# Order of four w3 transfers and of one V transfer in a one-core decode kernel

## The chip, the cores and the metric

The kernel runs on one core of a Trainium2 chip. A core has a matrix engine (PE, with its weight loads shown as PEld), a vector engine (DVE), an activation engine (ACT), GpSimd (POOL) and a sync engine (SP), and 16 DMA engines that bring data from HBM into its on-chip memory of 128 partitions. DMAs are issued by instructions on SP, ACT or POOL. The metric is the time of one execution on the device in microseconds, lower is better. The time before is 530.65 us, the median of three runs (530.46 to 531.92).

## What is computed

One decode step of a transformer block for four sequences, with attention and a gated feed-forward part in parallel on the same normalised input, both added to x:

```python
x = A_x                                   # 4 x 1 x 640, bf16
xn = _layernorm(x)
# attention: 32 heads of 192, the last W = 2048 of 8192 cached positions
q = x @ wq                                # 640 x 6144
scores = einsum("bhqd,bhkd->bhqk", q, k) * 192 ** -0.5
o = einsum("bhqk,bhkd->bhqd", softmax(scores), v)
attn = o.reshape(B, Sq, 6144) @ wo        # 6144 x 640
# feed-forward
h = silu(xn @ w1) * (xn @ w3)             # w1, w3: 640 x 1536
ffn = h @ w2                              # 1536 x 640
return x + attn + ffn
```

There is little arithmetic for each byte: the windows of K and V are 3 MiB per head each, 64 such tiles, and each byte is used once.

## The kernel before

**Tiles.** For one head, K and V of the window are tiles of 128 partitions (32 position groups by 4 sequences) of 64 positions by 192 numbers, 24,576 bytes in a partition. `load_k` and `load_v` bring one tile each by a DMA issued on SP; `load_v` can cut it into parts along the positions. There are two K buffers and three V buffers, so K of head h waits until the four multiplies on K of head h-2 are done, and V of head h until the matmuls of `pv` for head h-3 are done.

**Work on a head.** It is cut into four units, 128 in all (NU). For each unit DVE multiplies a quarter of K with the broadcast query (`mult`, line 246), PE adds up over slices of the head dimension with an identity matrix (`adder`, line 257), DVE reduces to scores (`reduce_quarter`, line 265). Four units on, a short chain gives the maximum, the exponentials and the masked weights z (lines 269 to 301); `pv` (line 309) is 32 matmuls of z with V, and `ge_sum`, `ge_turn` and `ge_proj` (lines 334 to 348 and 233) sum, divide, turn and project with wo, a group of four heads at a time.

**Order.** The order of instructions on each engine is written by hand: `add(slot, phase, function, ...)` puts work into a slot, and the loop at the end emits the slots in order, within a slot by phase. Issues of DMAs have phase 0. SP executes its issues in that order, and an issue that waits for its buffer holds those behind it. K of head h is issued in slot 4(h-1), V of head h in slot 4h+2, up to head 28. The last ones are different. K31 is in slot 120 (NU-8), V29 in slot 121 (NU-7), and slot 122 (NU-6) has V30, V31 in two parts, the first part of w2, the last two parts of wo and two small parts of w2. So SP's order at the end is K29, V28, K30, K31, V29, V30, V31a, V31b, w2, wo, wo, w2, w2.

**w3.** w1 comes early on SP. w3 comes through GpSimd's queue in slot 24, into the buffer of w1, as four DMAs (`ffn_load_split`, lines 362 to 370). A reset of the queue's cursor goes first. The 640 rows of w3 are spread unevenly over the partitions: partitions 0 to 63 hold four rows each, partitions 64 to 127 hold six. `SPLIT` (line 184) has the two kinds in the order four, six; each DMA fills 32 partitions, and the source is viewed as 8 by 4 partitions. So the four DMAs are: four rows to partitions 0 to 31 (384 KB), six rows to 64 to 95 (576 KB), four rows to 32 to 63, six rows to 96 to 127. The matmuls that read w3 (line 377) are in slot 31. The first part of w2 uses the same buffer after it.

## Time and profile before

| what | value |
|---|---|
| median of three runs | 530.65 us |
| the profiled execution, whole | 530.28 us |
| its span, first to last instruction | 528.5 us |
| bytes moved by DMA, mean rate | 223.31 MB, 423 GB/s |
| busy share of the span | PE 68%, DVE 66%, PEld 27%, ACT 8%, POOL 1% |
| chain that ended last | DMA 65%, DVE 22%, PE 11%, ACT 1% |
| median time from issue to landing | K 18.8 us, V 26.3 us |

The profile is of one execution. Its lists say, for every instruction, when it started, how long it took, and what ended the idle time before it. The chain of waits goes back from the last instruction, at each step to what released it. Views by windows give, for a stretch of the span, each engine's busy time, the granted PE clock, the busy share of the 16 DMA engines (a packet counts where it starts, so a short window can show over 1) and GB/s. DMA queues have numbers: q1 is SP's, q0 is GpSimd's, q10 is ACT's, q8 and q14 carry instructions. The trace also has a record of each DMA packet (start, duration, bytes, queue), which does not name the DMA engine.

### The profile page before, as it was taken

The numbers are of one execution on the slowest core, as the hardware profiler recorded it, in microseconds if no ns is written. First come the engines' busy times: TensorE is split into PE (matmuls) and PEld (weight loads), VectorE is DVE, ScalarE is ACT, GpSimd is POOL, SyncE is SP. The second block draws the span as 40 slices with busy tenths as digits, with TensorE's granted clock in tenths as the row PEclk, the third lists the DMA queues.
The fourth block names the chain that finished last, engine by engine and source line by source line (L and its number), as shares of the span: only waits on it lengthen the run. The fifth ranks groups of instructions, "written<-read, shape, count | busy, mean of one in ns | idle before, by whom it ended". The sixth has DMA issues, their size and how long they took to land.

```text
span 528.5 us, 5466 instructions
## 1 busy us (share of the span) xinstructions
PE 358.2 (68%) x2316; PEld 142.8 (27%) x2317; DVE 346.8 (66%) x445; ACT 44.3 (8%) x142; POOL 3.4 (1%) x12
## 2 busy tenths in 40 slices
PE   2766638686756766667738768576686867685774
PEld 1322213232222322222213323232232322232232
DVE  4179545787577767686646877477657876776940
ACT  2121000000000000000000000000000000000010
POOL 0001000000000000000000000000000000000000
PEclk9989787889878999798897988799878898889999
DMA  8999999999999999999999999999999999999995
GB/s 358 435 427 440 417 432 443 424 438 427 432 433 430 433 428 433 429 433 431 432 435 430 430 430 432 432 435 432 433 423 439 427 435 427 435 429 400 422 406 214
DMA packets 11888, 223.31 MB, mean 423 GB/s; under 512 B 1484, under 2 KB 1624, under 8 KB 2776
## 3 DMA queue, kind: packets, MB, share of 16 engines
q1 hardware_dynamic: 11528, 221.00, 97.7%
q0 software_dynamic: 320, 1.97, 0.9%
q8 instruction: 18, 0.29, 0.2%
q14 instruction: 6, 0.05, 0.0%
q10 hardware_dynamic: 16, 0.01, 0.0%
HBM read 222.96 MB, written 0.01 MB: 422 GB/s over the span
## 4 chain that ended last, share of the span: by engine, by line
DMA 65%; DVE 22%; PE 11%; ACT 1%; issue 1%; SPq 0%
DMA kt<-in_A_k_cache_dram 55%; DVE pr L246 15%; DMA w<-in_B_w_dram 6%; PE ps L257 6%; DMA wt<-in_A_wq_dram 4%; DVE sc L265 3%; PE po L334 2%; PE qps L212 1%; DVE z L301 1%; ACT ex L293 1%; DVE oT L342 1%; PE mt L287 0%; DVE og L339 0%; DVE qbc L218 0%; PE mt L274 0%
## 5 line engine op out<-in xcount | busy, mean ns | idle before, releaser
L257 PE MATMUL ps<-pr,idb 128*128 128x512 bf16 x768 | 215.5, 423 | 148.3 <-DVE pr L246 148.2
L246 DVE TENSOR_TENSOR pr<-kt,qbc 128x3072 bf16<-128x3072 bf16 x128 | 223.4, 1746 | 109.0 <-DMA kt<-in_A_k_cache_dram 109.0
L257 PEld LDWEIGHTS <-idb 128*128 128x128 bf16 x768 | 75.6, 103 | 256.1 <-issue 200.1
L265 DVE TENSOR_REDUCE sc<-ps 128x16 f32<-128x512 f32 x128 | 87.1, 681 | 2.4 <-PE ps L257 2.4
L309 PE MATMUL o_ps<-vt,z 128*8 128x384 bf16 x1024 | 56.2, 351 | 0.6 <-DMA vt<-in_A_v_cache_dram 0.6
L334 PE MATMUL po<-o_sb,sel_w 128*32 128x192 f32 x128 | 49.2, 518 | 1.1 <-ACT o_sb L316 1.1
L309 PEld LDWEIGHTS <-z 128*8 128x8 bf16 x1024 | 25.2, 90 | 30.1 <-issue 19.5
L316 ACT COPY o_sb<-o_ps 128x384 f32<-128x384 f32 x32 | 15.3, 478 | 189.0 <-PE o_ps L309 189.0
L301 DVE TENSOR_TENSOR z<-ex,mask_b 128x256 bf16<-128x256 bf16 x32 | 13.5, 422 | 23.9 <-ACT ex L293 23.9
L290 ACT COPY negm<-mt 128x1 f32<-128x1 f32 x32 | 5.1, 159 | 244.5 <-PE mt L287 244.5
L334 PEld LDWEIGHTS po<-o_sb,sel_w 128*32 128x32 f32 x128 | 13.8, 130 | 28.7 <-issue 26.9
L212 PE MATMUL qps<-wt,xnT 128*128 128x512 bf16 x59 | 16.1, 429 | 3.4 <-DMA wt<-in_A_wq_dram 3.3
L218 DVE CAST qbc<-qps 128x512 bf16<-128x512 f32 x6 | 3.8, 684 | 16.3 <-PE qps L212 16.3
L279 DVE TENSOR_REDUCE gmax<-mt 1x4 f32<-1x128 f32 x32 | 8.8, 275 | 6.9 <-PE mt L274 6.9
L287 PEld LDWEIGHTS mt<-ones_ff,gneg 1*128 1x128 f32 x64 | 9.4, 182 | 13.8 <-issue 10.4
L287 PE MATMUL mt<-ones_ff,gneg 1*128 1x1 f32 x64 | 12.1, 256 | 0.0
L274 PE MATMUL mt<-idf,lmax 128*1 128x128 f32 x32 | 11.2, 351 | 1.1 <-DVE lmax L269 1.1
L293 ACT ACTIVATE ex<-sc,negm 128x64 bf16<-128x64 f32 x32 | 11.1, 348 | 1.0
L233 PE MATMUL acc<-wo_t,oT 128*4 128x320 bf16 x96 | 9.2, 298 | 2.3 <-DMA wo_t<-in_A_wo_dram 2.3
L212 PEld LDWEIGHTS <-xnT 128*128 128x128 bf16 x60 | 6.4, 107 | 12.7 <-issue 7.6
L321 PEld LDWEIGHTS po<-rsum,tot_w 128*32 128x32 f32 x64 | 4.5, 108 | 13.3 <-issue 12.7
L269 DVE TENSOR_REDUCE lmax<-sc 128x1 f32<-128x64 f32 x32 | 7.0, 220 | 1.1
(63 smaller groups left out, 67.6 us busy)
## 6 DMA issues: line engine op xcount, KB each, us to landing
kt<-in_A_k_cache_dram SPq DMA_DIRECT2D x32, 3072.0 KB, 18.8
vt<-in_A_v_cache_dram SPq DMA_DIRECT2D x31, 3072.0 KB, 26.3
wo_t<-in_A_wo_dram SPq DMA_DIRECT2D x8, 960.0 KB, 20.8
wt<-in_A_wq_dram SPq DMA_DIRECT2D x2, 3072.0 KB
vt<-in_A_v_cache_dram SPq DMA_DIRECT2D x2, 1536.0 KB, 31.8
w<-in_B_w_dram SPq DMA_DIRECT2D x1, 1920.0 KB, 37.0
wt<-in_A_wq_dram SPq DMA_DIRECT2D x1, 1536.0 KB, 19.9
w<-in_B_w_dram SPq DMA_DIRECT2D x1, 1280.0 KB, 34.4
```

Of the source, the lines that this page charges most:

```text
L212: nc.tensor.matmul(qp[:], lhsT=xnT[:, kc].rearrange("p a b -> p (a b)"), rhs=wq_rows[kc][:, (c0 + i) * QC:(c0 + i + 1) * QC], start=(kc == ...
L233: nc.tensor.matmul(acc[i * CT:i * CT + B, :], lhsT=lhsT, rhs=rhs[:, i * N0:(i + 1) * N0], start=first, stop=last)
L246: nc.vector.tensor_tensor(out=pr[:], in0=kts[h][:, g * JQ:(g + 1) * JQ, :], in1=qbc[:, h * Dh:(h + 1) * Dh].unsqueeze(1).to_broadcast([P, ...
L257: nc.tensor.matmul(ps[:], lhsT=idb[:], rhs=pr[:, :, kk * DD:(kk + 1) * DD], start=(kk == 0), stop=(kk == NK - 1))
L265: nc.vector.tensor_reduce(out=scs[h][:, g * JQ:(g + 1) * JQ], in_=pss.pop(u)[:], axis=AX.X, op=ALU.add)
L274: nc.tensor.transpose(out=mt[0:1, 0:P], in_=chs[h][0][:], identity=idf[:])
L287: nc.tensor.matmul(mt[:, P:P + 1], lhsT=gneg[:].rearrange("o p b -> o (p b)"), rhs=ones_ff[0:1, 0:1], start=True, stop=True)
L293: nc.scalar.activation(out=ex[:], in_=scs.pop(h)[:], func=ACTF.Exp, bias=negm[:, 0:1], scale=SCALE, accum_out=rsum[:])
L301: nc.vector.tensor_tensor(out=z[:], in0=ex[:].unsqueeze(2).to_broadcast([P, NJ, B]), in1=mask_b[:].unsqueeze(1).to_broadcast([P, NJ, B]), ...
L309: nc.tensor.matmul(o_ps[c * CT:c * CT + 2 * B, :], lhsT=z[:, 2 * jj:2 * jj + 2, :], rhs=vt[:, 2 * jj:2 * jj + 2, :], start=(jj < 4), stop= ...
L316: nc.scalar.copy(out=o_sb[:], in_=o_ps[:])
L334: nc.tensor.matmul(po[sl, 0:Dh], lhsT=sel_w[:, par].rearrange("p a b -> p (a b)"), rhs=o_sb[:, par * Dh:(par + 1) * Dh].rearrange("p (r i) ...
```

## The change

Two things are reordered; no instruction computes anything else.

- `ffn_load_split` goes through `SPLIT` in reverse order, so that the first and third of GpSimd's four DMAs are the six-row parts (partitions 64 to 95 and 96 to 127) and the second and fourth are the four-row parts.
- `load_v` takes a range of positions. V29 is loaded in two halves: the first in slot 118 (4 x 29 + 2), ahead of K31 in slot 120, the second in slot 121, where the whole of V29 was. V30 and V31 keep their places and their parts. SP's order at the end becomes K29, V28, K30, V29a, K31, V29b, V30, V31a, V31b, w2, wo, wo, w2, w2.

```diff
-    def load_v(h, parts=1):
-        vt = vpool.tile([P, NJ, Dh], BF16, tag="vt")
+    def load_v(h, j0=0, j1=NJ):
+        if j0 == 0:
+            vts[h] = vpool.tile([P, NJ, Dh], BF16, tag="vt", name="vt")
         src = v_win[:, h].rearrange("b (p j) d -> p b j d", p=PB)
-        n = NJ // parts
-        for j in range(0, NJ, n):
-            nc.sync.dma_start(out=vt[:, j:j + n, :].rearrange("q j d -> q (j d)"),
-                              in_=src[:, :, j:j + n, :].rearrange("p b j d -> p b (j d)"))
-        vts[h] = vt
+        nc.sync.dma_start(out=vts[h][:, j0:j1, :].rearrange("q j d -> q (j d)"),
+                          in_=src[:, :, j0:j1, :].rearrange("p b j d -> p b (j d)"))
...
         for g in range(HP // CT):
-            for p0, d0, kn in SPLIT:
+            for p0, d0, kn in SPLIT[::-1]:
...
-        if h < H - 2:
-            add(u0 + 2 if h < H - 3 else NU - 7, 0, load_v, h)
+        if h < H - 3:
+            add(u0 + 2, 0, load_v, h)
+        elif h == H - 3:
+            add(u0 + 2, 0, load_v, h, 0, NJ // 2)
+            add(NU - 7, 0, load_v, h, NJ // 2, NJ)
...
-    for h in range(H - 2, H):
-        add(NU - 6, 0, load_v, h, 1 + (h == H - 1))
+    add(NU - 6, 0, load_v, H - 2)
+    add(NU - 6, 0, load_v, H - 1, 0, NJ // 2)
+    add(NU - 6, 0, load_v, H - 1, NJ // 2, NJ)
```

## The prediction

> **What bounds the kernel now.** I read the page first: the DMA slices are full from end to end, and DVE at 66% and PE at 68% are far from it.

> ```profile
> DMA  8999999999999999999999999999999999999995
> ...
> q1 hardware_dynamic: 11528, 221.00, 97.7%
> q0 software_dynamic: 320, 1.97, 0.9%
> q8 instruction: 18, 0.29, 0.2%
> ```

> The reader sees the bound in the first line, and in the others who shares the 16 DMA engines: the SP queue (q1) with nearly all bytes, the four w3 transfers of GpSimd (q0), and 18 fetches of instructions (q8). Next the chain of waits (start, us, what):

> ```profile
> 480.16 11.83 DMA kt<-in_A_k_cache_dram
> 492.01 32.52 DMA w<-in_B_w_dram
> 524.58 0.73 PE acc L233 x8
> ```

> The last three steps are the landing of K31, the landing of the last part of w2 at 524.58, and PE work of 0.7 us. So the end follows the last DMA. How evenly that last DMA ends is in the windows view of half microseconds (the last two columns are the busy share of the DMA engines and GB/s):

> ```profile
> 520.50:521.00 0.50, 0.00 (x0) 0.00 (x0) 0.00 (x0) 0.00 (x0) 0.00 (x0) 1.00 0.96 389
> 521.00:521.50 0.50, 0.33 (x6) 0.24 (x7) 0.00 (x0) 0.00 (x0) 0.00 (x0) 1.00 0.72 284
> 521.50:522.00 0.50, 0.50 (x10) 0.29 (x7) 0.00 (x0) 0.00 (x0) 0.00 (x0) 1.00 0.45 184
> ...
> 522.50:523.00 0.50, 0.00 (x0) 0.00 (x0) 0.00 (x0) 0.00 (x0) 0.00 (x0) 1.00 0.37 146
> ...
> 523.50:524.00 0.50, 0.50 (x10) 0.31 (x11) 0.00 (x0) 0.00 (x0) 0.00 (x0) 1.00 0.12 49
> ...
> ```

> Up to 521 us nearly all engines work, at 521.75 seven of 16 (0.45), at 522.75 six, in the last microsecond two (0.12). Two engines set the end, over 3 us behind the first. The question is what made them late.

> **A ledger of the 16 engines.** The trace keeps each DMA packet's start, duration, bytes and queue, not its engine. The engines can be strung together all the same: a 24,576-byte packet takes 912 ns, the next on its engine starts 3 to 4 ns before its end, and every engine must meet its share (8 of 128 rows, then a 4-byte packet) of each SP transfer in the order of issue. That gives 16 unbroken chains; chains may be confused where two run in step, so halves are safer than single engines. They show:
> - Each w3 transfer lies on eight engines only: the four-row parts (12,288-byte packets, 460 ns, four per engine and transfer) on one half, the six-row parts (18,432 bytes, 686 ns) on the other. Two transfers of four packets at 0.226 us more make that half 8 x 0.226 = 1.81 us late. I call the halves light and heavy.
> - A 16,384-byte fetch holds its engine 0.95 us and lengthens its neighbour from 0.91 to 1.39, 1.42 us in all (at 299.9 us, for one). The 18 fetches go round eight engines, six heavy and two light. An 8,192-byte fetch (q14) costs 0.83.
> - Except at one place the chains show no gap above 0.15 us between 20 us and the end, so lateness stays. When K30's share lands, measured from the engine furthest ahead (478.98 us in the span), the light half is late by 0, 0.12, 0.13, 0.53, 0.86, 2.29, 2.93 and 2.98 us, the heavy one by 2.15, 2.84, 4.89, 4.95, 5.04, 5.05, 5.07 and 5.35. Two heavy engines get one more fetch after that, at 496.8 and 516.6 us.
> - The one place is where K31 waits for its buffer: the light engines have run dry.

> ```profile
> 479.00:481.00 2.00, 1.01 (x7) 0.59 (x7) 1.73 (x2) 0.00 (x0) 0.00 (x0) 1.00 0.69 295
> 481.00:483.00 2.00, 2.00 (x35) 0.81 (x34) 0.00 (x0) 0.00 (x0) 0.00 (x0) 1.00 0.88 319
> ...
> ```

> From K30's landing to the end of w2 an engine that never idles takes 39.03 us (the heavy engine with 5.35: 484.33 to 523.36). The model's last engine is then 478.98 + 5.07 + 39.03 + 1.42 = 524.50; the trace has 524.59. The ledger closes within 0.1 us.

> **The change, part by part.**
> *w3's order.* The same four transfers and bytes. If the halves follow the position in the sequence, the light half now carries 1.81 us more and the heavy one 1.81 less. Lateness at K30: 1.81, 1.93, 1.94, 2.34, 2.67, 4.10, 4.74 and 4.79 on the first half, and 0.34, 1.03, 3.08, 3.14, 3.23, 3.24, 3.26 and 3.54 on the second. With a last fetch of 1.42 on those of 3.24 and 3.26 the second half ends at 4.68, so 4.79 on the first is last. Its end is 478.98 + 4.79 + 39.03 = 522.80, against 524.50 by the same sum: 1.70 us earlier. w3 itself landed by 72 us and is read at 145.8 us, so its own landing has 73 us of cover.

> [...]

> [...]

> *Half of V29 ahead of K31.* V29's buffer is free when pv of head 26 is done, at 471.2 us (the PE matmuls of 468.94), after K30's issue at 466.69 and before the light engines run dry at 479. So V29a issues with no wait of its own that delays K31, whose release is the multiply ending at 480.1. V29a costs each engine 8 x 0.457 = 3.66 us, which fills the gap (dry from 479.3, K31's first packets at 481.6). This ends the idling of engines that are not last, so it is worth 0 at the end; the 16 half packets for eight whole ones and one more 4-byte packet cost 16 x 0.4565 - 8 x 0.9083 = 0.04 us. From both sides: the two rows above lose 2 x 0.31 + 2 x 0.12 = 0.86 us of all engines' time, the most that filling them could bring if the last engine were among the idle ones (none of the late ones has a gap there); and the 12,288-byte packets of V31a ran 0.66 us slow as a group while those of V31b did not, so at worst two halves cost 1.3. I take 0.05, nearest to V31b's row and the w3 rows.

> *What K31 delays.* K31's bytes now queue behind V29a. The last engine's K31 lands at 478.98 + 4.79 + 3.66 + 7.27 = 494.7; a multiply starts 0.42 us after its landing (484.33 to 484.75), so 495.1.

> ```profile
> 484.75 1.76 DVE L246 TENSOR_TENSOR pr<-kt,qbc 128x3072 bf16<-128x3072 bf16 x1 [4.01 <-DMA kt<-in_A_k_cache_dram]
> ...
> 493.86 1.75 DVE L246 TENSOR_TENSOR pr<-kt,qbc 128x3072 bf16<-128x3072 bf16 x1
> ...
> 496.13 1.75 DVE L246 TENSOR_TENSOR pr<-kt,qbc 128x3072 bf16<-128x3072 bf16 x1
> ```

> K31's first multiply is at 496.13. K30 lands 0.56 earlier (5.35 becomes 4.79), which moves it to 495.6, so K31 is 0.4 us early: no new wait. V29 whole lands at 478.98 + 4.79 + 14.6 = 498.4, before its matmuls at 504.5. The w2 issues that wait for earlier landings (at 492.0 and 500.4 before) move by under 3 us, ahead of packets due at 519.

> *The sum.* Span 528.5 - 1.70 + 0.05 = 526.8 us; the 3.9 us from last landing to end stay. The profiled execution took 530.28, so 528.6; the median of the runs, 530.65, is 0.37 above that: 528.9 us, 0.32% less.

> **The rivals.**
> (1) *The halves follow the partitions.* For it: partitions 0 to 63 got the four-row parts and 64 to 127 the six-row parts, so today's packets can't tell the two readings apart. Against it: line 364 resets a cursor ahead of the four transfers, which would be idle if nothing moved on with each. Time: 530.65 + 0.05 = 530.7.
> (2) *The fetches go round from another place.* 18 fetches on eight engines leave two with a third one. If one falls on a fetching engine of the first half, that ends at 4.79 + 1.42 = 6.21, i.e. 524.2 against 524.5: 530.65 - 0.3 = 530.4. For it: one of the three runs shown, 531.92, is 1.3 above the others, about one fetch. Against: the other three executions lie within 0.4 us.
> (3) *The slower one: the fetching engines are really in the light half.* My chains name no engine; if the fetches and the six-row parts are on opposite halves today, the swap puts them together and the last engine gains the whole 1.81: 530.65 + 1.81 = 532.5. It decides as soon as the engine that lands last belongs to today's light half. For it: only the stringing of chains tells. Against: fetches on the light half last 881 to 886 ns and the others 921 to 967, two kinds that fit the halves exactly, and a tail of seven engines over 1 us long is what a heavy half with fetches would leave.

> **How the numbers follow.** Forecast 0.68, (1) 0.11, (2) 0.09, (3) 0.12. The forecast's own range is 528.0 to 529.6 (half a microsecond for the runs' scatter, 0.66 once for slow half packets). A measurement can tell 0.3%, 1.6 us: below 529.06 is faster. The forecast lies 0.15 us under that bound; a fast fetch order or less scatter brings more, so I give it 0.53 faster and 0.15 same. With (1) and (2) same is 0.35, slower is (3), 0.12. The range reaches from 528.0 to 530.9 over (1) and (2) and leaves out (3).

> **What would show it.** Right: the w3 packets of 18,432 bytes come first on q0; no share under 0.9 between 479 and 483 us; the last landing near 522.9 with more than two engines busy in its last microsecond; the multiply of 496.13 not waiting for K31. Wrong: a tail as long as before with the last landing at 524.6 (1 or 2) or 526 (3), or DVE idle for K31 by more than 0.5 us.

## The result, and the profile after

The kernel after takes 539.94 us (median of 6 runs, 537.14 to 540.19); the kernel before, run beside it, 530.35. The ratio is 1.0166, 95% interval 1.0143 to 1.019: 8.8 us slower, where 1.7 us faster was forecast. The profiled execution took 540.19 us, its span 538.4.

The page of after shows where. The slices are 13.46 us each:

```profile
DMA  8999999999999999999999999999999999999994
GB/s 356 433 436 407 285 268 419 436 434 436 422 438 428 433 430 432 434 427 428 431 432 433 435 435 427 435 436 422 434 429 433 434 433 428 433 436 431 428 421 183
...
q0 software_dynamic: 320, 1.97, 1.4%
```

The engines are as busy as before, from end to end. But in slices 4 to 6 (40 to 81 us) they move 407, 285 and 268 GB/s, where every later slice but the last is at 419 or more. Measured against 430, (23 + 145 + 162) x 13.46 / 430 = 10.3 us are lost there, which covers the whole loss. GpSimd's queue moved the same 320 packets and 1.97 MB, but they held 1.4% of the engines' time instead of 0.9%. The windows view of that stretch (the last two columns are the share and GB/s), first before, then after:

```profile
50.00:60.00 10.00, 3.47 (x42) 1.60 (x42) 5.15 (x6) 0.48 (x1) 0.00 (x0) 0.88 1.00 430
60.00:70.00 10.00, 8.11 (x30) 3.04 (x29) 8.17 (x11) 0.60 (x3) 0.00 (x0) 0.78 1.01 432
70.00:80.00 10.00, 3.86 (x41) 1.54 (x39) 3.36 (x4) 0.48 (x1) 0.00 (x0) 0.73 1.00 425
```

```profile
40.00:50.00 10.00, 7.20 (x49) 3.14 (x47) 9.50 (x11) 1.75 (x3) 2.27 (x4) 1.00 1.01 433
50.00:60.00 10.00, 5.72 (x46) 2.09 (x44) 3.29 (x4) 1.10 (x4) 0.00 (x0) 0.83 1.01 293
60.00:70.00 10.00, 5.08 (x13) 1.58 (x13) 6.32 (x8) 0.00 (x0) 0.00 (x0) 0.51 1.01 304
70.00:80.00 10.00, 6.12 (x53) 2.74 (x52) 3.98 (x5) 1.08 (x4) 0.00 (x0) 0.97 1.05 270
80.00:90.00 10.00, 1.60 (x4) 0.54 (x4) 3.38 (x4) 0.00 (x0) 0.00 (x0) 0.54 0.98 409
```

A share of 1.0 at two thirds of the rate (1.01 at 293 GB/s, where it was 1.00 at 430) goes with packets that last longer. In the packet records the w3 packets start between 51.0 and 80.6 us (before: 50.6 and 70.7). The 18,432-byte packets took 686 to 1,298 ns, median 1,136, where before all took 686; the 12,288-byte packets 576 to 872, median 778, where before they took 460 to 464. The 24,576-byte packets of K and V beside them are as bad, with a median of 1,442 ns instead of 912. So it isn't w3 alone that is slow: nine of ten packets that run with it are.

DVE is where the delay is felt. Its waits for K in the timeline (in brackets the idle time and what ended it) are 9.15 and 10.96 us there, where the same two were 4.85 and 6.64. The multiply is line 246 of the kernel before and line 244 of the kernel after; before comes first:

```profile
57.88 1.76 DVE L246 TENSOR_TENSOR pr<-kt,qbc 128x3072 bf16<-128x3072 bf16 x1 [4.85 <-DMA kt<-in_A_k_cache_dram]
...
76.61 1.76 DVE L246 TENSOR_TENSOR pr<-kt,qbc 128x3072 bf16<-128x3072 bf16 x1 [6.64 <-DMA kt<-in_A_k_cache_dram]
```

```profile
63.11 1.76 DVE L244 TENSOR_TENSOR pr<-kt,qbc 128x3072 bf16<-128x3072 bf16 x1 [9.15 <-DMA kt<-in_A_k_cache_dram]
...
86.58 1.76 DVE L244 TENSOR_TENSOR pr<-kt,qbc 128x3072 bf16<-128x3072 bf16 x1 [10.96 <-DMA kt<-in_A_k_cache_dram]
```

From there on the delay is carried. By the chains of packets, the first part of wo has landed on its last engine at 78.4 us before and 88.4 after; K30 at 484.3 and 494.3. The end of the chain of waits:

```profile
476.12 22.12 DMA vt<-in_A_v_cache_dram
498.26 34.12 DMA wo_t<-in_A_wo_dram
532.42 2.85 PE acc L231 x20
535.30 0.48 DVE res L475
```

The last packet of w2 ends at 533.54 (524.59 before), 8.95 later, so the last stretch gave back 1.0 us of the ten. PE then took the microsecond away again: twenty matmuls in 2.85 us, because the granted clock was 0.50 there against 1.00 before.

The stretch around K31, where the second edit works, went as forecast:

```profile
479.00:481.00 2.00, 0.00 (x0) 0.00 (x0) 0.90 (x1) 0.00 (x0) 0.00 (x0) 1.00 1.01 426
481.00:483.00 2.00, 1.09 (x6) 0.49 (x6) 1.97 (x4) 0.00 (x0) 0.00 (x0) 1.00 1.00 430
```

The same work comes ten microseconds later in this kernel, but its 488 to 496 us are full too, with shares of 0.93 to 1.05: nothing idles ahead of K31.

### The profile page after: what moved, and what is told of

Read it like the earlier page. It is cut to its first block, busy times and chain, and to the rows that moved or that the text cites. A ratio compares the mean times of both kernels' runs of the same rounds, so it can differ in the third digit from the quotient of the medians.

```text
span 538.4 us, 5467 instructions
## 1 busy us (share of the span) xinstructions
PE 360.2 (67%) x2316; PEld 143.7 (27%) x2317; DVE 346.6 (64%) x445; ACT 44.4 (8%) x142; POOL 3.4 (1%) x12
## 3 DMA queue, kind: packets, MB, share of 16 engines
q1 hardware_dynamic: 11672, 221.00, 97.1%
q0 software_dynamic: 320, 1.97, 1.4%
## 4 chain that ended last, share of the span: by engine, by line
DMA 65%; PE 19%; DVE 13%; ACT 2%; issue 1%; SPq 0%
DMA kt<-in_A_k_cache_dram 52%; PE ps L255 11%; DVE pr L244 10%; DMA wo_t<-in_A_wo_dram 6%; DMA vt<-in_A_v_cache_dram 4%; PE po L332 4%; DMA wt<-in_A_wq_dram 3%; PE qps L210 2%; DVE sc L263 2%; ACT ex L291 1%; DVE z L299 1%; PE mt L285 1%; PE acc L231 1%; PE mt L272 0%; ACT negm L288 0%
## 5 line engine op out<-in xcount | busy, mean ns | idle before, releaser
L210 PE MATMUL qps<-wt,xnT 128*128 128x512 bf16 x59 | 17.6, 464 | 2.5 <-DMA wt<-in_A_wq_dram 2.4
```

The source lines that it names most:

```text
L210: nc.tensor.matmul(qp[:], lhsT=xnT[:, kc].rearrange("p a b -> p (a b)"), rhs=wq_rows[kc][:, (c0 + i) * QC:(c0 + i + 1) * QC], start=(kc == ...
```

## The experiments

**w3's order alone.**

```diff
-            for p0, d0, kn in SPLIT:
+            for p0, d0, kn in SPLIT[::-1]:
```

> The kernel before with w3's six-row parts first and third; V29 whole, behind K31. Theory P (each DMA engine writes one fixed set of partitions for SP's transfers; the new order gives w3 parts to engines of the other half, so two engines write the same partitions at once): all of the loss is here, +9 to +10 us against before, in 40 to 85 us of the span, with w3 packets of 18,432 bytes over 1 us. Rival V (the half of V29 ahead of K31 costs it): within 1 us of before.

540.69 us, ratio 1.0177 (1.0155 to 1.0199). All of the loss is in this line; V falls.

**The half of V29 alone**, which is the kernel after with `SPLIT[::-1]` turned back into `SPLIT`.

> The kernel after with w3 in the old order; half of V29 ahead of K31. Theory P: within 0.5 us of before; the DMA engines no longer idle between 479 and 483 us, and K31's first multiply still doesn't wait more than 0.5 us. Rival V: +8 us or more.

529.6 us, ratio 0.9981 (0.9971 to 0.9991): 1.0 us faster, twice what was allowed. The stretch ahead of K31 is full and K31's first multiply, the second of the two lines, starts without a wait for K31, as expected (timeline and windows of this run):

```profile
479.00:481.00 2.00, 1.00 (x7) 0.62 (x7) 1.78 (x2) 0.00 (x0) 0.00 (x0) 1.00 0.99 424
481.00:483.00 2.00, 2.00 (x36) 0.79 (x33) 0.00 (x0) 0.00 (x0) 0.00 (x0) 1.00 1.04 442
```

```profile
494.26 1.75 DVE L244 TENSOR_TENSOR pr<-kt,qbc 128x3072 bf16<-128x3072 bf16 x1
496.53 1.75 DVE L244 TENSOR_TENSOR pr<-kt,qbc 128x3072 bf16<-128x3072 bf16 x1
```

**Turning the sequence by eight engines, order kept.** One DMA of 16 KB in the same 8-by-4 form, in which each w3 part lies on eight engines by the chains, goes ahead of the four parts:

```diff
         nc.gpsimd.inc_swdge_sem([], [], mode="reset_dge_cursor")
+        pad = const.tile([CT, 256], BF16, name="pad")
+        nc.gpsimd.dma_start(out=pad[:], in_=w[0:CT, 0:256].rearrange("(b a) n -> a b n", a=8))
         for g in range(HP // CT):
```

> The kernel before plus one small GpSimd DMA (32 partitions of 512 bytes, source viewed as 8 by 4 rows) ahead of the four w3 parts; their order, sizes and partitions stay. If GpSimd's DMAs take engines in turn, this moves each w3 part by eight engines. Theory P: +9 to +10 us, w3 packets as slow as in the kernel after. Rival S (the order of sizes is what hurts, six-row packets ahead of four-row ones): within 0.5 us of before. If the parts follow the partitions and not the turn: within 0.5 us too.

543.33 us, ratio 1.0227 (1.0204 to 1.0249). The order, the sizes and the partitions of w3 are untouched, and yet the kernel is 12 us slower, because 16 KB went ahead. S falls, and so does the idea that the parts follow their partitions: here position decides. The loss is 2 us over the expectation.

**The same DMA ahead of the kernel after's order.**

> The kernel after plus the same small GpSimd DMA ahead of the four w3 parts. Theory P: each part is back on the engines of its own partitions, so the loss goes: 529.5 to 531 us, w3 packets at 460 and 686 ns. Rival S: as slow as the kernel after, 540 us.

530.01 us, ratio 0.9989 (0.9978 to 1.0). The loss is gone, and all 128 w3 packets take 460 and 686 ns again. The 30 us around w3 in these two runs, first the slowed one, then the mended one:

```profile
50.00:80.00 30.00, 13.78 (x106) 5.71 (x106) 13.31 (x16) 1.55 (x5) 0.00 (x0) 0.83 1.02 269
```

```profile
50.00:80.00 30.00, 15.23 (x110) 6.18 (x110) 16.44 (x20) 1.56 (x5) 0.00 (x0) 0.82 1.01 433
```

The share is 1.0 in both. An extra DMA slows one kernel and heals the other.

**Six rows on partitions 0 to 63, issued first.** The two kinds change partitions, and the lines that build and read w3's layout follow (200 to 204 and 375 to 378):

```diff
-    SPLIT = [(0, 0, KL), (HP, HP * KL, KH)]
+    SPLIT = [(0, HP * KL, KH), (HP, 0, KL)]
...
-        nc.tensor.transpose(out=xsT_ps[HP:P, k, :], in_=xs[:, c0:c0 + HP], identity=idb[0:B, 0:B])
+        nc.tensor.transpose(out=xsT_ps[0:HP, k, :], in_=xs[:, c0:c0 + HP], identity=idb[0:B, 0:B])
...
-            q0 = 0 if k < KL else HP
+            q1 = P if k < KL else HP
...
```

> The kernel before with w3 turned over: six-row parts on partitions 0 to 63 and issued first and third, four-row parts on 64 to 127; V29 whole. Size order and load of the two halves of engines are those of the kernel after, but each part is on the engines of its own partitions. Theory P: no w3 packet over 700 ns, and the balance that the prediction counted on shows: -1.0 to -1.8 us against before. Rival S (the order of sizes hurts): +9 us. Rival L (loading the first half of the engines more hurts): slower than before.

530.2 us, ratio 0.9989 (0.9979 to 0.9998), so 0.1 to 1.1 us faster. All packets take 460 and 686 to 689 ns. Size order and loads are those of the kernel after, without its loss: S falls a second time, and L with it. The gain is at or under the low end of what was expected.

**Four rows on partitions 64 to 127, issued first**: the same layout with the two entries of `SPLIT` exchanged.

> As the run with six rows on partitions 0 to 63, but the four-row parts (partitions 64 to 127) are issued first and third, as in the kernel before; so size order and engine loads are those of before, and only the partitions are crossed. Theory P: +9 to +13 us. Rival S: as before, within 1 us.

544.81 us, ratio 1.0266 (1.0248 to 1.0284): 14 us slower, with order and loads those of before and only the partitions crossed. Rival S would have it as before. That crossing with the four-row parts first costs 12 to 14 us, and with the six-row parts first 9 to 10 (the kernel after, counted without what half of V29 gains it, among them), in two kernels each, was not expected, and nothing here says why.

**Both edits without the crossing**: six rows on partitions 0 to 63, first, and half of V29 ahead of K31.

> Six-row parts on partitions 0 to 63 and issued first and third, and half of V29 ahead of K31: both edits of the kernel after, without the crossing. Theory P: both gains, -2.0 to -2.8 us against before, 527.8 to 528.6 us: faster than both kernels. If the balance of the halves is worth nothing: as the run with V29 alone, -1.0 us.

528.77 us, ratio 0.9965 (0.9953 to 0.9977): 1.9 us faster than before, 11 us faster than the kernel after, and the fastest kernel of the study, just short of what was expected. Its tail in windows of a microsecond:

```profile
520.00:521.00 1.00, 0.15 (x4) 0.00 (x0) 0.00 (x0) 0.00 (x0) 0.00 (x0) 1.00 0.44 173
521.00:522.00 1.00, 0.00 (x0) 0.00 (x0) 0.00 (x0) 0.00 (x0) 0.00 (x0) 1.00 0.30 120
522.00:523.00 1.00, 0.85 (x12) 0.53 (x12) 0.00 (x0) 0.00 (x0) 0.00 (x0) 1.00 0.11 41
523.00:524.00 1.00, 0.83 (x8) 0.35 (x7) 0.00 (x0) 0.00 (x0) 0.00 (x0) 0.58 0.01 5
```

The last packet of w2 ends at 523.26 instead of 524.59. By the packet records a single engine has packets left from 522.4 us on; the one after it in lateness ends 0.9 us earlier.

**Turning by two engines.** As the turn by eight, with `a=2` in the small DMA.

> The kernel before plus a small GpSimd DMA on two engines ahead of the four w3 parts, so that the parts move by two engines instead of eight. If every engine has partitions of its own (theory P): all four-row packets and a quarter of the six-row packets are on foreign partitions, 55% of w3's bytes, so +4.5 to +7 us and nearly all 12,288-byte packets over 460 ns. Rival H (only the two halves of 64 partitions matter): a quarter of the bytes cross, +2 to +3.5 us, and most 12,288-byte packets stay at 460 ns.

539.94 us, ratio 1.0172 (1.0157 to 1.0186): 9.1 us slower. Only 3 of 64 four-row packets and 6 of 64 six-row packets stay within 15 ns of 460 and 686. H, which allows 3.5 us and most packets unslowed, falls: a turn by two costs 9.1 us where the one by eight, in the same order of parts, costs 12. It is also worse than P's own estimate of 4.5 to 7 us. That the small DMA with `a=2` takes two engines was assumed, and no run shows it. Either it takes others, or the shares of a part lie on the engines in another order than assumed, or the stalls spread; that wasn't told apart.

**A probe with nothing beside it.** After w2's last landing, w3 is loaded twice more into a K buffer that is no longer needed, and nothing reads it:

```diff
+    probe = kpool.tile([P, NJ, Dh], BF16, tag="kt", name="probe")
+    nc.gpsimd.tensor_copy(out=probe[:, 0, 0:2], in_=ffn["w2"][:, FC - 1, D - 2:D])
+    for parts in (SPLIT, SPLIT[::-1]):
+        for g in range(HP // CT):
+            for p0, d0, kn in parts:
...
+                nc.gpsimd.dma_start(out=probe[q0:q0 + CT].rearrange("p j d -> p (j d)")[:, 0:kn * F], in_=src)
```

> The kernel before with eight more GpSimd DMAs after the last landing of w2, when SP's queue is empty: w3 again into a K buffer that is no longer needed, first the four parts in the order of before (own partitions), then, once these have landed, the four in the order of the kernel after (foreign partitions). Nothing reads them; the time grows by the probe alone and says nothing else. Theory P as contention (two engines writing the same partitions): both rounds run at the same pace, 460 and 686 ns a packet or both with the same scatter, since no other traffic is there. Rival R (the way from an engine to foreign partitions is slow by itself): the second round's packets are slow, 700 to 1,200 ns, as in the kernel after.

546.41 us, which includes the probe. GpSimd's timeline shows the copy that waits for w2, the first round, and the second, each pair of DMAs behind the landing of the parts that it writes over, so that the rounds overlap by 1.2 us:

```profile
525.38 0.18 POOL L472 COPY probe<-w 128x2 bf16<-128x2 bf16 x1 [476.83 <-DMA w<-in_B_w_dram]
525.91 2.12 POOL L478 DMA_DIRECT2D probe<-in_B_w_dram  x4 [0.35 <-POOL probe L472]
533.05 1.10 POOL L478 DMA_DIRECT2D probe<-in_B_w_dram  x2 [5.03 <-DMA probe<-in_B_w_dram]
536.46 1.10 POOL L478 DMA_DIRECT2D probe<-in_B_w_dram  x2 [2.31 <-DMA probe<-in_B_w_dram]
```

By the packet records, in the round on own partitions 43 of 64 four-row and 51 of 64 six-row packets stay within 15 ns of 460 and 686; in the round on foreign partitions 47 and 43. The medians are 460 and 686 in both. The slow ones come mostly where a DMA begins, in both rounds. So R falls: with no other traffic the crossing shows no cost in these medians. In every run with a loss (269 to 297 GB/s between 50 and 80 us) K and V packets ran beside it. Whether the two kinds of packets meet at the partitions or on a way to them that both use wasn't told apart. That the second round is the crossed one follows from the turns and isn't seen in a record.

## Why the prediction was wrong

**The chains and the turn: right.** The reading that before's end is set by the two DMA engines with the most bytes and fetches holds, as does the reading that position in GpSimd's sequence picks the half. In after's chains six of the eight engines with 16,384-byte fetches are in the half that now carries the four-row parts; before, they were in the half of the six-row parts. The lengths of the fetches say the same: the short ones, of the other two engines (881 to 886 ns before, 879 to 896 after), were with the four-row parts before and are with the six-row parts now. So these engines stayed and the parts moved. Rival (1), the halves follow the partitions, falls by this and by the two turns by eight (543.33 and 530.01 us). In the ledger's lists two engines stand in the wrong half: the one late by 2.29 us is of the heavy half and the one late by 2.84, with two of the short fetches, of the light half. No maximum changes by it.

**The step that failed** is "w3's order. The same four transfers and bytes." It kept 460 and 686 ns for the packets on the other half's engines and asked only when the last engine ends. The prediction wrote itself, under rival (1), that "today's packets can't tell the two readings apart", position and partition half going together in the kernel before, and used it only to leave that rival open. It did not ask what happens when they part. What happens is 10 us: 30 us in which the rate is 270 to 304 GB/s instead of 430, with the 18,432-byte packets at a median of 1,136 ns instead of 686. None of the rivals had it. The slower one (3) was about which half fetches, at 1.8 us.

How far the runs bear P out: the turn by eight brought a loss of 12 us to before's order (543.33 us) and took the loss from after's (530.01), as P has it. The turn by two agrees less, with 119 of 128 packets slow where 55% of the bytes were expected on foreign partitions. The records name no engine, so the pairs themselves stay inferred.

**The balance of the halves: right mechanism, size off.** Forecast -1.70 us. Measured without the crossing: 0.6 us (0.1 to 1.1) with V29 whole, and with V29 halved the step from 0.9981 to 0.9965, 0.9 us (about 0 to 1.7, from two sets of runs). The mis-sized term is the lateness of the last engine. The one of 4.74 us that carries the small fetches gets one more of 0.83 near the end (at 518.2 us before), which the prediction's sum leaves out. In after's chains it is the last one, 5.57 us behind the first at the last part of wo. 4.74 + 0.83 = 5.57 is 0.78 over the 4.79 of the sum, and 1.70 less 0.78 is 0.9. PE took some too: the granted clock fell to 0.58 in the microsecond after 523 us and to 0.50 behind it in the best kernel, and its last eight matmuls took 1.23 us instead of 0.71.

**V29 ahead of K31: put at a cost of 0.05 us, worth a gain of 1.0 us (0.5 to 1.5).** It fills the idle stretch and brings K31 in time, both as worked out: K31's first multiply waits 0 us in two of the four profiles with V29a ahead and 0.4 in the other two. The gain goes with a row that the prediction had seen and used as a possible cost, the 0.66 us by which V31a ran slow; in the run with V29 alone the last packet of w2 ends 0.6 us earlier than before. In all seven profiles in which the engines idle ahead of K31, 58 to 76 of the late half-V packets are over 470 ns, 0.43 to 0.65 us for each engine. In three of the four profiles with V29a ahead it is one packet, and none of V31. In the fourth, the kernel after with the turn, it is 44 and 0.3 us, but 38 of them are of V29 and only six of V31. So but for these six the slow packets of V31 come with the idling; that the idling causes them isn't shown, and how it could is open.

**Luck in the total.** The best kernel takes 528.77 us, and the forecast was 528.9. That is luck: the balance was put too high by 0.8 to 1.1 us and the half of V29 too low by about as much.

**After in sum.** The w3 stretch adds 10.0 us (first part of wo, last engine). The last packet of w2 is 8.95 late, so the two gains together gave back 1.0. PE at half clock took 1.0 again between that packet and the final copy (1.76 us against 0.74). The span is 9.9 longer.

## What to carry to other kernels

When transfers of two queues share DMA engines, ask for each which engines it runs on and, since P fits most of these runs, which partitions those engines write for the other queue. Order and one small extra DMA on GpSimd's queue decided it here: 16 KB ahead of the sequence cost 12 us in before's order and took away the loss of 9 to 10 in after's. The sign was a full busy share at a lower rate (1.01 at 293 GB/s, 1.00 at 430 before); then look at how long single packets last, 1,442 ns here instead of 912. And before costing a reordering at "the same bytes", write down what goes together in the old order by construction, and what the new one separates.

## What the runs showed of the hardware that was not expected

- With w3's 1.97 MB on GpSimd's queue in the new order, nine of ten K and V packets beside them were slow for 30 us, with a median of 1,442 ns instead of 912. That the engines write other partitions for SP is inferred.
- With no other traffic beside it, the crossed round's medians were 460 and 686 ns, those of the uncrossed one.
- Idle engines ahead of K31 were followed 25 us later by half-V packets that, together, ran 0.43 to 0.65 us long on each engine (seven profiles of seven). With the idle stretch filled, V31 had none of them in three profiles and six in the fourth.
- The granted clock was 0.50 from 532 us to the end of PE's work in the kernel after, and 1.00 in the last microseconds before: twenty matmuls took 2.85 us after, 1.7 before.
